# Fewer blocks first, a product pass of four tiles, and mixing on VectorE in a fused RWKV-5 and shrink-MLP kernel

## The chip, the cores and the metric

The kernel runs on one core of a Trainium2 chip. The metric is the device time of one execution in microseconds (us); lower is better. A core has five engines that run their own instruction streams: TensorE (PE, matmuls; its weight loads are listed as PEld), VectorE (DVE), ScalarE (ACT), GpSimd (POOL) and SyncE (SP, which here only issues transfers). The profile is that of one execution.

## The reference

All arithmetic is float32. `r`, `k`, `v` are (4, 8, 768, 48): 4 sequences, 8 heads, 768 steps, 48 per head.

```python
# first block: a decayed linear attention with a bonus for the own step
for t in range(S):
    cur = einsum('bhd,bhe->bhde', u[None] * k[:, :, t], v[:, :, t])
    y[:, :, t] = einsum('bhd,bhde->bhe', r[:, :, t], state + cur)
    state = w[None, :, :, None] * state + einsum('bhd,bhe->bhde', k[:, :, t], v[:, :, t])
x = y.transpose(0, 2, 1, 3).reshape(3072, 384)
# second block, w_in (384, 2048) and w_out (2048, 384), both given as float64
h = x @ w_in
out = (h - tanh(h)) @ w_out
```

## The kernel before, in words

**Units.** The first block is cut into 24 units of 64 steps of two sequences with all heads. For a unit SyncE loads r, k and v; TensorE transposes r and k (`turn`), multiplies the two for the levels (`levels`, with the state's part in `from_state`), VectorE masks the levels (`x.cp`, a predicated copy, L892), ScalarE writes the diagonal (`diagonal`), and TensorE multiplies by v (`outputs`) and updates the state (`to_state`), all of them recorded on L693. ScalarE copies the result to `xt`, and GpSimd issues small transfers that move the rest into place (`fill`). The first units have TensorE banks of their own (`x_ps`); the later ones, called `two` in the code, share one pair of banks (`yk_ps`), so their steps follow one another more strictly.

**Blocks and tiles.** Two units make a block of 256 rows of x; there are 12 blocks. The second block of the reference runs block by block over 8 tiles of 256 columns of w_in. A tile is: h, two halves of three matmuls each (L166); five ScalarE steps on 128x512 (`s`, `th`, `tg`, `q`, `small`); four VectorE steps on 128x512 (`g`, `c1`, `c2`, `cp`, L190 to L196), which make g = h - tanh(h) with a series where h is small; and the multiplication of g by its rows of w_out. A tile does this plainly (`o`, L204: four matmuls of 384 columns) or with seven products for eight (`products`, L254): g is cut into four 128x128 squares and w_out into 192-column halves, as in Strassen's scheme in Winograd's form; seven matmuls of 192 columns take the place of eight. The products need three sums of the squares of g (`sums_of_g`, GpSimd, L239 to L243) and four combinations of the squares of w_out (`mix`, GpSimd, L263, sixteen instructions for all of w_out, made once). `collect` (L275, L284) combines the seven results after a block's last tile.

**Passes.** The first FIRST = 6 blocks go through the tiles in four passes of two tiles each (PASSES = 4, 4, 4, 4 counts columns of 128), so that work can begin while w_in and w_out are still on their way; a block's sums wait in `part` (L217 adds them up). The other six blocks go through all eight tiles at once with `products`, except the last two tiles of the last block (ALONE = 4), which are plain.

**Weights.** w_in and w_out come as 64-bit words in 16 pieces; VectorE (L135, L136, L139 to L141, on 128x768) and ScalarE (L137, L138) convert each piece, and four staging buffers hold pieces on the way. The products' combinations lie where the staging buffers were, so mixing waits for all 16 conversions (`converted` in `mixing`).

**Order.** Nothing runs in the order in which the code names it. `Plan` holds every step with an engine, an assumed cost, what it waits for and a due time; `forward` lists the steps by due time on each engine, `order` searches over due times, and the steps are then issued in the order of the best plan. The plan also assumes when TensorE's own instructions arrive (`step`, `bound`, `comes`), and puts filler matmuls that compute nothing of use into the gaps at the start (`fills`, `filled`; L630 and L631), so that TensorE's clock stays up. In `order` the gaps are computed a second time, from a step's start and cost.

Of the kernel before, what the change touches and what calls it, by code (L numbers as in the profile page):

```python
# [34 lines left out]
L = 2  # L35
FIRST = 6
PASSES = 4, 4, 4, 4
OWN = 1
SWAP = 2
ALONE = 4  # L40
# [103 lines left out]
class Dense:  # L144
# [62 lines left out]
    def empty(self, t, i):  # L207

        whole, at = t.fs[1] == self.d.NF, (t.j, i)
        if t.fs[0]:  # L210
# [3 lines left out]
            if i and t.j in self.negative:  # L214
                self.nc.vector.tensor_tensor(t.o, part, self.outs[i], ALU.subtract)
            else:
                self.nc.vector.tensor_tensor(t.o, self.outs[i], part, ALU.add)  # L217
# [39 lines left out]
    def mix(self, f, x):  # L257
# [5 lines left out]
        self.nc.gpsimd.tensor_tensor(pairs[:, :, out], a, b, op)  # L263

    def collect(self, t, x):

        n, ps, V = self.d.DM // 2, self.seven.ps, self.nc.vector
        if x == 0:
            t.e, t.u = (self.work.tile([128, self.d.DM], F32, name=name, tag="part", bufs=L * FIRST) for name in "eu")
            whole = t.fs[1] == self.d.NF  # L270
            t.os = [self.work.tile([128, self.d.DM], F32, name="o", tag="o") if whole else
                    self.work.tile([128, self.d.DM], F32, name="part", tag="part", bufs=L * FIRST) for _ in range(L)]
            if not whole:
                self.sums.update({(t.j, i): t.os[i] for i in range(L)})
            self.nc.scalar.copy(t.e[:, :n], ps[0][:, :n])  # L275
        else:
# [7 lines left out]
            V.tensor_tensor(out, x, y, op)  # L284

# [10 lines left out]
class Plan:  # L296
# [33 lines left out]
    def forward(self, due):  # L330
# [7 lines left out]
        starts, done, last, first, changed = [None] * len(ready), [], 0.0, {}, set(waiting)  # L338
        while len(done) < len(ready):
# [21 lines left out]
            if e == "PE":  # L361
                if filling:
                    step += 4 * len(self.filled(filling, free[e], start, starts))
# [72 lines left out]
    def order(self, tries=1000):  # L436
# [24 lines left out]
        free, order, fills = self.BEGIN["PE"], [], iter(self.fills)  # L461
        filling = next(fills, None)
        for t in done:
            t.start = starts[t.n]
            if t.engine == "PE" and filling:
                order += [SimpleNamespace(engine="PE", cost=0.0, start=free, run=run)
                          for run in self.filled(filling, free, t.start, starts)]
                if t is filling[1]:
                    filling = next(fills, None)
                free = t.start + t.cost  # L470
# [21 lines left out]
def near(ctx, tc, r, k, v, w, u, out, shared, moe_w_in, moe_w_out):  # L492
# [75 lines left out]
    def new_outs(t):  # L568
        if t.j >= FIRST:
            return [x[:, : d.DM] for x in dense.seven.ps[:L]]  # L570
# [22 lines left out]
    dense.negative = set(range(FIRST, d.NB))  # L593
# [34 lines left out]
    def fills(to):  # L628
        wide = w_up.rearrange("d p z t -> d (p z t)")
        return [(.9, lambda: T.matmul(to, ident, wide, start=True, stop=True)),  # L630
                (.25, lambda: T.matmul(to[:, :128], ident, ident, start=True, stop=True))]  # L631
# [280 lines left out]
    def mixing():  # L912

        for f in range(0, d.NF // 2, 2):
            now = None
            for x in range(4):
# [4 lines left out]
                now = add("POOL", 1.0, run, converted + [now])  # L921
            mixed.append(now)

    def finished_seven(t, x, due, pace):

        whole, now, steps, j = t.fs[1] == d.NF, x.o, [], t.j
        for i, (e, cost) in enumerate((("ACT", .3), ("DVE", .26), ("DVE", .26), ("DVE", .26), ("DVE", .26), ("DVE", .47), ("DVE", .26))):
            now = add(e, cost, lambda i=i: dense.collect(t, i), [now] + (sum((stored.get((j - 1, i), []) for i in range(L)), []) if whole and not i else []), due + 3 * pace)
            steps.append(now)
        x.empty, x.emptied = steps[:4], steps[4:]  # L930
        if whole:
            for i in (1, 0):
                stored[j, i] = [add("POOL", .6, lambda z=z, i=i: dense.store(t.os[i], L * j + i, z, G),
                                    [steps[4 if i else 6]], due + 4 * pace, data=.4) for z in range(2)]

    def hidden(j, fs, f, due, pace, seven=False):
# [10 lines left out]
        if m == 0:  # L947
            plan.fills += [([], tabled, fills(idle)[1:]), ([ups], now, fills(idle))]
# [9 lines left out]
        if seven:  # L958
# [4 lines left out]
            now = add("PE", 1.32, lambda: dense.products(t, 0), [x.sg, mixed[f // 4], b1.o, done.cp, done.diag, done.lev] + b1.empty, due + 2 * pace, steps=16)  # L963
            x.o = add("PE", .99, lambda: dense.products(t, 1), [now] + b1.emptied, due + 2 * pace + 1.3, steps=12)
            if t.last:
                finished_seven(t, x, due, pace)
# [360 lines left out]
```

## Time and profile before

| | |
|---|---|
| Median of the runs | 617.49 us (3 runs, 616.53 to 619.28) |
| The profiled execution | 616.69 us, its span 615.0 us |
| Mean granted TensorE clock | 0.991 |
| TensorE busy | 596.4 us (97%) |
| Weight loads (PEld) | 483.4 us (79%) |
| VectorE busy | 453.5 us (74%) |
| ScalarE busy | 401.9 us (65%) |
| GpSimd busy | 177.1 us (29%) |
| h, L166 | 282.4 us busy, 1152 records |
| Plain w_out, L204 | 142.0 us busy, 384 records of 400 |
| Seven products, L254 | 158.6 us busy in four groups, 644 records |
| Mixing, L263 | 22.0 us busy in three groups, 16 instructions |

A float32 matmul shows as two records. A group's busy time is the time in which at least one of its records runs; records of matmuls overlap, so the time that one takes is read from start to start. A busy TensorE need not be at its peak. A few matmul records are missing. Timeline lines give start and length in us, engine, line, operation, output and inputs, shapes and count; in brackets the idle time before and what ended it. Lines of stretches give, for each engine, busy us and count, then TensorE's granted clock, the busy share of the transfer engines and GB/s.

### The profile page before, as it was taken

The numbers are of one execution on the slowest core, as the hardware profiler recorded it, in microseconds if no ns is written. First come the engines' busy times: TensorE is split into PE (matmuls) and PEld (weight loads), VectorE is DVE, ScalarE is ACT, GpSimd is POOL, SyncE is SP. The second block draws the span as 40 slices with busy tenths as digits, with TensorE's granted clock in tenths as the row PEclk, the third lists the DMA queues.
The fourth block names the chain that finished last, engine by engine and source line by source line (L and its number), as shares of the span: only waits on it lengthen the run. The fifth ranks groups of instructions, "written<-read, shape, count | busy, mean of one in ns | idle before, by whom it ended". The sixth has DMA issues, their size and how long they took to land.

```text
span 615.0 us, 13927 instructions
## 1 busy us (share of the span) xinstructions
PE 596.4 (97%) x5499; PEld 483.4 (79%) x5499; DVE 453.5 (74%) x735; ACT 401.9 (65%) x896; POOL 177.1 (29%) x313
## 2 busy tenths in 40 slices
PE   8799999999999999997999999999999999999995
PEld 7477777667777777775777799889889899889993
DVE  5599888997789689996668765766786765645753
ACT  2498878878676567662557765675775666747652
POOL 5001311300000000193123452543362244436440
PEclk9899999999999999997999999999999999999999
DMA  7964686407024100002123410130120010100101
GB/s 128 219 126 88 129 161 166 90 0 174 8 46 102 52 0 2 0 14 52 38 52 82 82 23 0 37 57 19 26 58 17 15 27 7 23 6 8 26 2 30
DMA packets 86323, 33.73 MB, mean 55 GB/s; under 512 B 78537, under 2 KB 80681, under 8 KB 86249
## 3 DMA queue, kind: packets, MB, share of 16 engines
q1 hardware_dynamic: 81084, 25.57, 20.7%
q0 software_dynamic: 4992, 6.99, 5.2%
q8 instruction: 45, 0.74, 0.5%
q14 instruction: 30, 0.24, 0.1%
q10 hardware_dynamic: 172, 0.20, 0.1%
HBM read 26.94 MB, written 4.72 MB: 51 GB/s over the span
## 4 chain that ended last, share of the span: by engine, by line
PE 79%; DVE 9%; ACT 5%; issue 3%; DMA 2%; SPq 1%; DVEq 0%; ACTq 0%
PE h L166 36%; PE p L254 17%; PE o L204 16%; PE yk_ps L693 5%; DVE rT L742 1%; DVE tg L194 1%; PE yk_ps L738 1%; DVE tg L192 1%; PE h L630 1%; SPq L726 1%; ACT at L763 1%; PE p L204 1%; PE x_ps L738 1%; DVE g L196 1%; DMA kt<-in_k_dram 1%
## 5 line engine op out<-in xcount | busy, mean ns | idle before, releaser
L166 PE MATMUL h<-xt,w_in_sb 128*128 128x256 f32 x1152 | 282.4, 382 | 0.2 <-DVE w_in_sb L141 0.2
L166 PEld LDWEIGHTS h<-xt,w_in_sb 128*128 128x128 f32 x1152 | 214.6, 191 | 42.7 <-issue 1.0
L204 PE MATMUL o<-w_out_sb,g 128*128 128x384 f32 x384 | 142.0, 493 | 0.5 <-DVE g L196 0.3
L192 DVE SCALAR_TENSOR_TENSOR tg<-s,tg 128x512 f32<-128x512 f32 x96 | 68.7, 716 | 58.8 <-ACT tg L179 44.4
L190 DVE TENSOR_TENSOR g<-h,th 128x512 f32<-128x512 f32 x96 | 65.9, 686 | 43.0 <-ACT s L175 32.2
L204 PEld LDWEIGHTS o<-w_out_sb,g 128*128 128x128 f32 x384 | 72.0, 191 | 32.5 <-DVE g L196 1.4
L179 ACT ACTIVATE tg<-h 128x512 f32<-128x512 f32 x96 | 57.2, 595 | 53.7 <-PE h L166 53.7
L175 ACT ACTIVATE s<-h 128x512 f32<-128x512 f32 x96 | 57.3, 596 | 49.7 <-PE h L166 49.7
L177 ACT ACTIVATE th<-h 128x512 f32<-128x512 f32 x96 | 57.1, 595 | 32.0 <-PE h L166 31.9
L196 DVE COPY_PREDICATED g<-small,tg 128x512 f32<-128x512 int32 x96 | 73.2, 763 | 5.0
L194 DVE SCALAR_TENSOR_TENSOR tg<-q,tg 128x512 f32<-128x512 f32 x96 | 69.6, 725 | 6.1 <-ACT q L181 2.6
L239 POOL TENSOR_TENSOR sg<-g 128x256 f32<-128x256 f32 x46 | 35.2, 766 | 132.3 <-DVE g L196 123.0
L181 ACT ACTIVATE q<-s,m1b 128x512 f32<-128x512 f32 x96 | 69.5, 724 | 0.5
L183 ACT ACTIVATE small<-s,smallb 128x512 f32<-128x512 f32 x96 | 69.4, 723 | 0.5
L254 PE MATMUL p<-mixed,sg 128*128 128x192 f32 x276 | 67.4, 326 | 0.0
L850 POOL DMA_DIRECT2D xt<-rest x66 | 32.4, 497 | 91.8 <-ACT rest L829 91.6
L763 ACT ACTIVATE at<-same,du 128x64 f32<-128x64 f32 x184 | 47.6, 341 | 4.9 <-DVE du L759 4.7
L254 PEld LDWEIGHTS p<-mixed,sg 128*128 128x128 f32 x276 | 48.7, 190 | 0.0
L254 PE MATMUL p<-w_out_sb,g 128*128 128x192 f32 x184 | 46.2, 333 | 0.0
L254 PEld LDWEIGHTS p<-w_out_sb,g 128*128 128x128 f32 x184 | 33.2, 190 | 4.3
L263 POOL TENSOR_TENSOR mixed<-w_out_sb 128x384 f32<-128x384 f32 x8 | 10.9, 1378 | 77.2 <-DVE w_out_sb L141 77.2
L829 ACT COPY xt<-yk_ps 64x192 f32<-64x192 f32 (+2 forms) x50 | 16.2, 323 | 23.7 <-PE yk_ps L693 23.3
(136 smaller groups left out, 694.4 us busy)
## 6 DMA issues: line engine op xcount, KB each, us to landing
st<-in_moe_w_out_dram SPq DMA_DIRECT2D x8, 768.0 KB, 7.3
rt<-in_r_dram SPq DMA_DIRECT2D x48, 96.0 KB, 2.9
vt<-in_v_dram SPq DMA_DIRECT2D x48, 96.0 KB, 3.0
st<-in_moe_w_in_dram SPq DMA_DIRECT2D x16, 288.0 KB, 6.4
kt<-in_k_dram SPq DMA_DIRECT2D x44, 96.0 KB, 2.9
out_dram<-part POOLq DMA_DIRECT2D x24, 96.0 KB, 2.2
out_dram<-o POOLq DMA_DIRECT2D x20, 96.0 KB, 2.1
st<-in_moe_w_in_dram POOLq DMA_DIRECT2D x16, 96.0 KB, 3.9
```

Source lines behind the costliest of these rows:

```text
L166: self.nc.tensor.matmul(t.h2[:, z], self.w_in_sb[:, t.f // 2, kk, z * 128 : (z + 1) * 128], self.xts[t.j][:, kk].rearrange("p b t -> p (b ...
L175: A.activation(out, t.h, AF.Square)
L177: A.activation(out, t.h, AF.Tanh)
L179: A.activation(out, t.h, AF.Tanh, scale=G1)
L181: A.activation(out, t.s, AF.Square, bias=self.m1b)
L183: A.activation(out, t.s, AF.Relu, bias=self.smallb, scale=-1.0)
L190: V.tensor_tensor(t.g, t.h, t.th, ALU.subtract)
L192: V.scalar_tensor_tensor(t.tg, t.s, C4, t.tg, ALU.mult, ALU.mult)
L194: V.scalar_tensor_tensor(t.tg, t.q, K1, t.tg, ALU.add, ALU.mult)
L196: V.copy_predicated(t.g, t.small.bitcast(I32), t.tg)
L204: self.nc.tensor.matmul(self.outs[i], t.g2[:, z, i * C : (i + 1) * C], self.w_out_sb[:, t.f + z, :], start=t.first and z == 0, stop=t.last ...
L254: self.nc.tensor.matmul(ps[bank][:, half * n : (half + 1) * n], a, b, start=t.first and half == 0, stop=t.last, skip_group_check=True)
```

## The change

It has six parts.

1. FIRST goes from 6 to 5. PASSES become 4, 4, 8: two passes of two tiles and one of four. In that last pass (columns from SEVEN = 8 on) the tiles use `products`. The sums of the first two passes wait in `part` as before, and a new function `gather` adds them to what `collect` makes of the third.
2. ALONE goes from 4 to 2: one plain tile at the end instead of two.
3. Mixing runs on VectorE instead of GpSimd, and is planned ahead of the passes, since the third pass needs it.
4. `collect` starts after the first four of a tile's seven products, and has its own buffers `e` and `u`. The products of the next tile wait for its first four steps, not for all.
5. A filler is 512 or 256 columns of the identity (before: 512 of the decay table, once that was there, or 128 of the identity), from the first instruction on. `order` takes the fillers from the plan that it chose (`fitted`), instead of computing the gaps again.
6. All blocks keep the second half of their x negated (`negative`), as the seven products want it; plain parts undo the sign when they are whole.

With it the first 14 units (before: 16) use the separate banks, and 10 (before: 8) share one pair. Of the 96 tiles 21 are plain (before: 50) and 75 use products (before: 46).

```diff
-FIRST = 6
-PASSES = 4, 4, 4, 4
+FIRST = 5
+PASSES = 4, 4, 8
-ALONE = 4
+ALONE = 2
+SEVEN = 8
...
-            if i and t.j in self.negative:
+            if i and whole and t.j in self.negative:
...
-        self.nc.gpsimd.tensor_tensor(pairs[:, :, out], a, b, op)
+        self.nc.vector.tensor_tensor(pairs[:, :, out], a, b, op)
...
+    def gather(self, t, i):
+        self.nc.vector.tensor_tensor(t.os[i], t.os[i], self.sums.pop((t.j, i)), ALU.subtract if i else ALU.add)
...
-                    step += 4 * len(self.filled(filling, free[e], start, starts))
+                    runs = self.filled(filling, free[e], start, starts)
+                    self.fitted.append((free[e], t.n, runs))
+                    step += 4 * len(runs)
...
-            if t.engine == "PE" and filling:
-                order += [SimpleNamespace(engine="PE", cost=0.0, start=free, run=run)
-                          for run in self.filled(filling, free, t.start, starts)]
-                if t is filling[1]:
-                    filling = next(fills, None)
-                free = t.start + t.cost
+            free, runs = fitted.get(t.n, (0.0, [])) if t.engine == "PE" else (0.0, [])
+            order += [SimpleNamespace(engine="PE", cost=0.0, start=free, run=run) for run in runs]
...
-    dense.negative = set(range(FIRST, d.NB))
+    dense.negative = set(range(d.NB))
...
-        wide = w_up.rearrange("d p z t -> d (p z t)")
-        return [(.9, lambda: T.matmul(to, ident, wide, start=True, stop=True)),
-                (.25, lambda: T.matmul(to[:, :128], ident, ident, start=True, stop=True))]
+        def run(n):
+            T.matmul(to[:, : n * 128].rearrange("p (n m) -> p n m", n=n), ident, ident[:, None, :].to_broadcast([128, n, 128]),
+                     start=True, stop=True)
+        return [(.9, lambda: run(4)), (.46, lambda: run(2))]
...
-                now = add("POOL", 1.0, run, converted + [now])
+                now = add("DVE", .47, run, converted + [now])
...
+            before = sum((stored.get((j - 1, i), []) for i in range(L)), []) if not i else [x.o] if i == 4 else []
+            now = add(e, cost, lambda i=i: dense.collect(t, i), [now] + before, due + 3 * pace)
             steps.append(now)
-        x.empty, x.emptied = steps[:4], steps[4:]
+        x.empty, x.emptied = steps[:2], steps[2:]
...
+            if t.fs[0]:
+                now = add("DVE", .47, lambda i=i: dense.gather(t, i), [now], due + 3 * pace)
...
-            plan.fills += [([], tabled, fills(idle)[1:]), ([ups], now, fills(idle))]
+            plan.fills.append(([], now, fills(idle)))
...
-            now = add("PE", 1.32, lambda: dense.products(t, 0), [x.sg, mixed[f // 4], b1.o, done.cp, done.diag, done.lev] + b1.empty, due + 2 * pace, steps=16)
+            now = add("PE", 1.32, lambda: dense.products(t, 0), [x.sg, mixed[f // 4], b1.o, done.cp, done.diag, done.lev] + b1.empty + b1.emptied[:2], due + 2 * pace, steps=16)
...
-                hidden(j, (done, done + part), f, now, pace)
+                hidden(j, (done, done + part), f, now, pace, done >= SEVEN)
```

## The prediction, made before the changed kernel ran

> **What bounds the kernel now.** I read the page's shares first (TensorE 97% busy, VectorE 74%, ScalarE 65%, GpSimd 29%), then the slices, because an average hides stages.
>
> ```profile
> PE   8799999999999999997999999999999999999995
> PEclk9899999999999999997999999999999999999999
> ```
>
> TensorE is full from the third slice on, except in the nineteenth, where its granted clock falls too. So time is TensorE's instructions, plus a few holes. Five places matter: the start (to 53 us, where the first w_out matmul stands), the hole near 283 us, the plain stage, the stage with products, the tail. Busy times by stretch, columns as in the page (PE, PEld, DVE, ACT, POOL, clock, DMA share, GB/s):
>
> ```profile
> 53.00:258.00 205.00, 203.62 (x1704) 150.25 (x1704) 177.29 (x287) 154.06 (x334) 18.62 (x38) 1.00 0.34 73
> 280.00:285.00 5.00, 1.65 (x42) 1.07 (x44) 4.74 (x8) 0.00 (x0) 1.54 (x3) 0.83 0.10 22
> 285.00:290.00 5.00, 5.00 (x44) 3.43 (x37) 1.12 (x2) 2.52 (x10) 1.03 (x2) 0.50 0.66 130
> ```
>
> From 53 to 258 us TensorE lacks only 1.4 us, but VectorE works 86% of it too: it also converts the weights. The hole, in the timeline:
>
> ```profile
> 258.96 2.73 POOL L263 TENSOR_TENSOR mixed<-w_out_sb 128x384 f32<-128x384 f32 x2 [77.16 <-DVE w_out_sb L141]
> 259.52 1.30 DVE L194 SCALAR_TENSOR_TENSOR tg<-q,tg 128x512 f32<-128x512 f32 x1
> ...
> 283.93 1.14 PE L693 MATMUL yk_ps<-at,vt 64*64 64x64 f32 x32 [3.35 <-DVE at L892]
> ```
>
> While the sixteen mixing instructions run on GpSimd (259 to 280 us, 22 us in all) VectorE's 512-wide steps take 1.3 to 1.5 us instead of 0.69. VectorE falls behind, TensorE waits 3.35 us, and then runs at half clock for 6.25 us, which costs another 3.1. The start and the tail:
>
> ```profile
> 20.20 0.77 PE L693 MATMUL x_ps<-rT,kT 48*64 48x64 f32 x26 [3.70 <-issue]
> 20.91 6.90 PE L630 MATMUL h<-w_up,ident 128*128 128x512 f32 x12
> ...
> 31.25 0.69 DVE L742 TENSOR_TENSOR rT<-x_ps,w_up 128x512 f32<-128x512 f32 x1 [3.48 <-ACT kT L751]
> ...
> 604.69 5.63 PE L204 MATMUL p<-w_out_sb,g 128*128 128x384 f32 x16 [1.66 <-DVE e L284]
> ```
>
> TensorE stands 3.7 us for nothing that the profile shows (my reading: its own instructions had not come), and then works off six filler matmuls in 6.9 us, half of them at half clock, though the operands of the next real matmuls were ready at 22.2. VectorE pays for it with 3.48 us of waiting.
>
> **The change, part by part.**
>
> *Products.* Steps from start to start:
>
> ```profile
> 348.19 1.45 PE L204 MATMUL o<-w_out_sb,g 128*128 128x384 f32 x4
> 349.48 1.46 PE L166 MATMUL h<-xt,w_in_sb 128*128 128x256 f32 x6
> 350.77 0.49 PE L254 MATMUL p<-w_out_sb,g 128*128 128x192 f32 x2
> ...
> 352.07 1.46 PE L166 MATMUL h<-xt,w_in_sb 128*128 128x256 f32 x6
> 353.37 0.49 PE L254 MATMUL p<-w_out_sb,g 128*128 128x192 f32 x2
> ...
> 354.34 1.46 PE L166 MATMUL h<-xt,w_in_sb 128*128 128x256 f32 x6
> ```
>
> Half a plain w_out tile takes 1.29 us, so a tile 2.58; four products take 1.30 and three 0.97, so a tile 2.27. Plain tiles go from 50 to 21 (20 in passes one and two, one at the end), product tiles from 46 to 75: 29 x 0.31 = **-9.0 us**. [...]
>
> Per product tile GpSimd adds three sums of g (0.77 + 0.53 + 0.56 = 1.86 us) in a period of 4.86: hidden, 177 busy us become about 209. Without that cover (sums later than the next half of h, 1.29 us) each tile would pay the excess. The cross-block collects on VectorE: six more at 1.78 (four 192-wide at 0.26 plus 0.26 and 0.47), ten gathers, minus 26 plain adds at 0.47: +3.2 us, and they lie in the product stage, where VectorE is 65% busy. A collect now starts after the first four products, and the next tile's first products wait for four of its steps (about 1.4 us) while three products and two halves of h (3.6 us) run: nothing. The ScalarE copy that begins a collect waits for the previous block's stores (2.1 us to land) with the next tile's tanh behind it, but blocks are 19 us apart: nothing.
>
> *Mixing on VectorE.* Sixteen instructions at the 0.47 of a 384-wide step, 7.5 us, and VectorE's other steps keep 0.61. The hole of 3.35 and its half clock go: **-6.4 us**. This holds where the hole stood; the mixing itself moves, see the third part.
>
> *Start.* Fillers become wide ones from the first instruction, and are set by what the plan assumed, so the six at 20.9 us become single ones. Against this, five 512-wide fillers now stand ahead of the transpose of decay and bonus (5.24 us before). A filler takes 0.86 us at full clock and 1.7 at half; a 128-wide one took 0.47 us from 1.5 us on and 0.22 from 7.8 on, so I put the rise near 6.9, and the five end near 8.5 and that transpose comes near 9.0, 3.7 us late. Stepping through the order, the second unit's first level matmuls then stand near 19.3 instead of 16.2. Before, they waited there until 20.2 anyway, so this costs nothing as long as the instructions arrive by then; bounds 0 to +5. After it one filler (0.9, cold 1.7) instead of 6.9 us lets the first half of h start near 26 instead of 30.9. From there VectorE sets the pace (21.4 of 22 us busy from 31 to 53): its order has 18.3 us of steps to the end of the first tile, so 45.5, and the first w_out matmul near 46.5 instead of 53.1: **-6.6 us**, between 0 and -9.
>
> *Earlier products: VectorE's queue.* All sixteen weight pieces and the first mixing must now be done before the first product, which moves from tile 49 to tile 21, while TensorE's work up to there shrinks. Steps of VectorE:
>
> ```profile
> 252.84 0.96 DVE L139 SCALAR_TENSOR_TENSOR w_out_sb<-w_out_sb,st 128x768 f32<-128x768 uint32 x1
> 253.70 0.69 DVE L194 SCALAR_TENSOR_TENSOR tg<-q,tg 128x512 f32<-128x512 f32 x1
> 254.30 0.56 DVE L217 TENSOR_TENSOR part<-o,part 128x384 f32<-128x384 f32 x1
> 254.77 0.95 DVE L140 SCALAR_TENSOR_TENSOR power<-st,power 128x768 uint32<-128x768 uint32 x1
> ```
>
> 0.86 for 768 wide, 0.60 to 0.61 for 512, 0.65 for a predicated copy, 0.47 for 384. Between the first tile's last step and the masking of unit 13 (the fourteenth), whose banks the products take over, VectorE's instructions in the order built from the changed program are 94 x 0.47 + 75 x 0.61 + 31 x 0.65 + 39 x 0.86 = 143.7 us. TensorE has, from its first w_out matmul to the first product, 132 x 0.431 (h) + 80 x 0.647 (w_out) + 608 small at 0.033 and 72 transposes at 0.11 = 136.7, and about 0.45 per unit for changes of shape (68.0 us measured for 63.5 of such work between the first and ninth tile), so 141. VectorE is the longer. Counted the same way, before had 173.0 us of VectorE steps in 205.8 us (84%), but there TensorE set the pace. Where VectorE was pressed it was 97% busy (31 to 53, 60 to 70 us). I take 96%: 149.7, so the first product near 195.2 instead of the 187.5 of TensorE alone: **+7.7 us**; bounds 0 (it keeps up) and +29 (84%). These gaps should be short and many. [...] One long gap would add 3 us, short ones nothing, and I take nothing.
>
> *Rest.* The small waits of 53 to 258 us (1.4) are inside the last item: -1.4. Two more units run with one shared bank pair in the product stage, where a unit cost 0.85 of changes (259.1 us from the first product to the end, for 250.6 of steps and the hole of 1.66, over eight units) instead of 0.45: +0.8. In the tail the last tile's chain (4.6 us from the end of h to its mask, as now) outlasts the 3.25 us of products left: a hole of 1.4 instead of 1.66: -0.3.
>
> **Sum**: -9.0 - 6.4 - 6.6 + 7.7 - 1.4 + 0.8 - 0.3 = -15.2. The profiled execution took 616.7 (span 615.0): 601.5; the median of the runs shown is 0.8 above it: **602.3 us**.
>
> **Rivals.**
> 1. *VectorE's queue becomes the bound and the kernel is slower.* Place: the first product. If VectorE gets through its 143.7 us at 84%, that product stands at 45.5 + 171 = 216.5, 21.3 later, total 623.6. For it: the 84%, and ScalarE, which shares the chain, was 86% busy from 31 to 121 us. Against: 97% where pressed. It decides below 143.7 / (149.7 + 15.2) = 87%.
> 2. *The hole wasn't the mixing's.* It is the long VectorE chain of a unit (masking behind four tile steps), and comes back before the first product with its half clock: +6.4, 608.7. For it: that unit waits at the head of TensorE's queue. Against: VectorE's doubled steps from 259 to 280.
> 3. *The start gains nothing.* The late transpose and the late instructions add up, the first w_out matmul stays near 53: 608.9. For it: the filler sum above. Against: VectorE's 3.48 us wait goes.
> 4. *VectorE keeps up* at 100%: 594.6.
>
> **How the numbers follow.** Forecast 0.50 (597 to 608), rival 4 0.14, rivals 2 and 3 together 0.24 (606 to 614), rival 1 0.12, of which two thirds end slower. A difference under 0.5% (3.1 us) can't be told from none here. Slower: 0.08; within: 0.05, the mild end of rival 1 and of 2 and 3 together; faster: 0.87. The range for 8 in 10 leaves out rival 1 and the best of rival 4: 594 to 613.
>
> **What would show it.** First w_out matmul near 46.5; first product near 195 with VectorE over 94% busy from 46 to 195 and TensorE's idle there 6 to 10 us in short gaps, ended by VectorE; no half clock after 30 us; product tiles at 4.86 from there on; 1.4 us of hole before the last w_out matmuls. Wrong if TensorE's idle before the first product is over 15 us or under 2, or if the first tile is not earlier.

## The result, and the profile after

| | before | after |
|---|---|---|
| Median | 618.27 us (4 runs, 616.53 to 619.28) | 610.81 us (4 runs, 610.4 to 611.83) |
| After to before | | 0.9885 (95%: 0.9856 to 0.9913) |
| Profiled execution, its span | 616.69, 615.0 us | 610.4, 608.7 us |
| TensorE / VectorE / GpSimd busy | 97 / 74 / 29% | 96 / 76 / 35% |
| First w_out matmul | 53.09 | 50.60 |
| First product | 350.77 | 197.59 |
| End of the last matmul; from there to the end of the span | 610.32; 4.65 us | 601.23; 7.45 us |

The kernel became 7.5 us faster; 15.2 were forecast (602.3 for 617.5). The time lies in the range of 594 to 613, and the sign was right, but half of the forecast gain isn't there; the range was wide enough for that, which is no merit of the working. Measured against the sum's own execution (a span of 599.8), 8.9 us are missing, and they can be placed:

| stretch | forecast | measured | difference |
|---|---|---|---|
| to the first w_out matmul | 46.5 | 50.6 | +4.1 |
| from there to the first product | 148.7 | 147.0 | -1.7 |
| from there to the end of the last matmul | 399.95 | 403.64 | +3.7 |
| from there to the end of the span (forecast as before) | 4.65 | 7.45 | +2.8 |

The slices of the changed kernel's page, busy TensorE and its granted clock in tenths:

```profile
PE   9789889999999989999999999999999999999994
PEclk9799999999999999999999999999999999999998
```

The hole in the nineteenth slice and its half clock are gone. In their place the third, fifth and sixth slices (30 to 46 and 61 to 91 us) are less full than the slices of before from the third on. TensorE's timeline at the start and at the first block with products (start, length, then as before):

```profile
1.52 6.01 PE L632 MATMUL h<-ident 128*128 128x512 f32 x10 [1.52 <-POOL ident masks.py:199]
...
7.90 0.23 PE L640 MATMUL yk_ps<-ident,rows 8*128 8x8 f32 x1
...
18.50 0.70 PE L632 MATMUL h<-ident 128*128 128x512 f32 x1
22.96 1.22 PE L632 MATMUL h<-ident 128*128 128x512 f32 x1 [3.76 <-issue]
...
29.45 1.46 PE L167 MATMUL h<-xt,w_in_sb 128*128 128x256 f32 x6
...
50.60 1.53 PE L205 MATMUL o<-w_out_sb,g 128*128 128x384 f32 x4 [0.76 <-DVE g L197]
```

```profile
197.59 0.59 PE L255 MATMUL p<-w_out_sb,g 128*128 128x192 f32 x2 [0.29 <-DVE at L896]
...
218.45 0.59 PE L255 MATMUL p<-w_out_sb,g 128*128 128x192 f32 x2 [0.93 <-DVE e L283]
...
220.18 0.59 PE L255 MATMUL p<-mixed,g 128*128 128x192 f32 x2 [0.81 <-DVE o L283]
```

The 3.7 us in which TensorE waits "for nothing that the profile shows" are still there, in the middle of one filler, and the first half of h comes at 29.45 instead of the forecast 26. At the end of the first block with products, TensorE waits 1.74 us for `collect`. The forecast had put the price of that wait at nothing: some 1.4 us of VectorE's steps against 3.6 us of TensorE's own work, with VectorE 65% busy in the stage with products. The stretches show why that average misled (columns as before):

```profile
200.00:225.00 25.00, 23.26 (x124) 21.15 (x123) 24.58 (x42) 13.81 (x31) 11.39 (x18) 1.00 0.08 17
225.00:250.00 25.00, 24.90 (x134) 23.01 (x133) 22.48 (x36) 14.83 (x28) 13.31 (x21) 1.00 0.11 25
250.00:275.00 25.00, 25.00 (x135) 23.31 (x134) 18.02 (x29) 16.21 (x30) 12.14 (x21) 1.00 0.08 17
```

VectorE is full until about 225 and 90% busy to 250, since mixing (185 to 211 us), the first collects and a unit meet there. The tail:

```profile
594.65 0.45 POOL L244 TENSOR_TENSOR sg<-sg,g 128x128 f32<-128x128 f32 x1
...
598.38 2.85 PE L205 MATMUL p<-w_out_sb,g 128*128 128x384 f32 x8 [0.36 <-DVE e L283]
```

The hole before the last w_out matmuls is 0.36 us (1.4 were forecast). But the span ends 7.4 us after the last matmul. In the trace's own records, which the page doesn't list since such steps don't count as busy, GpSimd has a last step (a drain) of 10.37 us after its last sum: from 597.48 to 607.84 in the changed kernel, from 599.77 to 610.14 before. Before, the other engines were done at 613.85 and GpSimd waited for them. After, they are done at 604.86 and wait 3.0 us for GpSimd.

### The profile page after: what moved, and what is told of

It reads as the page before. It is cut to its first block, busy times and chain, and to the rows that moved or that the text cites. A ratio compares the mean times of both kernels' runs of the same rounds, so it can differ in the third digit from the quotient of the medians.

```text
span 608.7 us, 14333 instructions
## 1 busy us (share of the span) xinstructions
PE 584.0 (96%) x5617; PEld 497.8 (82%) x5617; DVE 465.0 (76%) x771; ACT 403.4 (66%) x902; POOL 211.3 (35%) x384
## 4 chain that ended last, share of the span: by engine, by line
PE 69%; DVE 12%; ACT 8%; issue 7%; POOL 1%; DMA 1%; DVEq 0%; POOLq 0%; ACTq 0%
PE h L167 32%; PE p L255 24%; PE yk_ps L697 4%; PE o L205 4%; PE h L632 2%; DVE tg L193 1%; DVE tg L195 1%; DVE g L197 1%; DVE rT L746 1%; DVE g L191 1%; ACT th L178 1%; PE yk_ps L742 1%; ACT at L767 1%; POOL xt L854 1%; ACT s L176 1%
## 5 line engine op out<-in xcount | busy, mean ns | idle before, releaser
L240 POOL TENSOR_TENSOR sg<-g 128x256 f32<-128x256 f32 x75 | 57.0, 759 | 197.6 <-DVE g L197 142.6
L255 PE MATMUL p<-mixed,sg 128*128 128x192 f32 x450 | 110.1, 326 | 0.0
L255 PEld LDWEIGHTS p<-mixed,sg 128*128 128x128 f32 x450 | 79.3, 190 | 0.2 <-issue 0.2
L255 PE MATMUL p<-w_out_sb,g 128*128 128x192 f32 x300 | 74.9, 332 | 1.3 <-DVE e L283 0.9
L197 DVE COPY_PREDICATED g<-small,tg 128x512 f32<-128x512 int32 x96 | 71.2, 742 | 4.3
L255 PEld LDWEIGHTS p<-w_out_sb,g 128*128 128x128 f32 x300 | 54.9, 190 | 9.5 <-DVE e L283 1.3
L205 PE MATMUL o<-w_out_sb,g 128*128 128x384 f32 x160 | 59.1, 492 | 2.0 <-DVE g L197 1.2
L244 POOL TENSOR_TENSOR sg<-sg,g 128x128 f32<-128x128 f32 x75 | 44.4, 592 | 5.4
L205 PEld LDWEIGHTS o<-w_out_sb,g 128*128 128x128 f32 x160 | 29.3, 190 | 15.7 <-PE x_ps L632 1.6
L242 POOL TENSOR_TENSOR sg<-sg,g 128x128 f32<-128x128 f32 x75 | 40.2, 535 | 5.4
```

The source lines that it names most:

```text
L197: V.copy_predicated(t.g, t.small.bitcast(I32), t.tg)
L205: self.nc.tensor.matmul(self.outs[i], t.g2[:, z, i * C : (i + 1) * C], self.w_out_sb[:, t.f + z, :], start=t.first and z == 0, stop=t.last ...
L255: self.nc.tensor.matmul(ps[bank][:, half * n : (half + 1) * n], a, b, start=t.first and half == 0, stop=t.last, skip_group_check=True)
```

## The experiments

For comparison across kernels I split each profiled span into four parts. "Needed" is TensorE's instructions without fillers, at one duration for each kind (h 0.431, plain w_out 0.647, small 0.033 and transposes 0.110 us as in the prediction, a product 0.326). What is over before the first product (fillers, idle time, half clock, changes of shape) and after it is the rest of those stretches, and the last column is from the last matmul to the end.

| kernel | needed | over, before the first product | over, after it | end | span |
|---|---|---|---|---|---|
| before | 554.0 | 47.4 | 8.9 | 4.7 | 615.0 |
| after | 545.1 | 42.3 | 13.9 | 7.4 | 608.7 |
| after, profiled again (e15) | 545.1 | 44.7 | 13.9 | 7.2 | 610.9 |
| e4, mixing on GpSimd | 545.1 | 45.0 | 9.1 | 7.7 | 606.8 |
| e6, third pass plain | 551.2 | 38.7 | 9.8 | 8.1 | 607.8 |
| e9, VectorE relieved, planned | 545.0 | 39.5 | 10.8 | 7.6 | 602.9 |
| e10, VectorE relieved later | 545.1 | 42.0 | 10.9 | 7.4 | 605.3 |
| e11, old fillers and last sums | 545.1 | 41.2 | 12.6 | 4.8 | 603.5 |

Two profiles of the changed kernel differ by 2.4 us before the first product, so a difference of that size there proves nothing by itself. A second caution: where an experiment is "planned anew", `order` searches again (1000 random shifts, from a fixed start), so any change in what it is told can lead to another order of everything. e3, e4, e5, e6, e7, e8 and e9 are of this kind; e1, e2, e10, e13 and e14 keep the order of the changed kernel. No run changed the search alone, so what a new order is worth by itself isn't known; e3 and e7, whose edits concern the fillers of the start, gained 2.9 and 3.0 us. Ratios are to the kernel before on the same chip, with their 95% intervals.

**The end: e1, the last sums on VectorE.** The three sums of g of the last tile that uses products move; nothing else does.

```diff
-        add, g, s = self.nc.gpsimd.tensor_tensor, ...
+        add, g, s = (self.nc.vector if t.j == self.d.NB - 1 and t.f == self.d.NF - ALONE - 2
+                     else self.nc.gpsimd).tensor_tensor, ...
```

> The changed kernel with one edit: the three sums of g of the very last tile that uses products are made on VectorE instead of GpSimd; the planned order is kept. Theory (GpSimd's end): in the changed kernel GpSimd's last sum ends at 595.1, and after it stands a step of 10.37 us at its end, so that the program closes at 608.7, 3.0 us after the other engines are done. With the edit GpSimd is done one tile (4.9 us) earlier and no longer last: from the last matmul to the end of the span about 4.5 us instead of 7.5. The 0.8 us of sums that VectorE gets lie ahead of the last plain tile's steps, so up to 0.8 more of a hole there. Median near 608.2 (607.5 to 609). Rival (the end waits for the landing of the last transfers, or for SyncE): no gain, 610.8 to 611.6.

Measured: 609.25 us, ratio 0.9834 (0.9809 to 0.986). From the last matmul to the end it is 4.7 us; GpSimd's drain, again 10.37 us, runs from 594.69 to 605.06. So the place is confirmed. The median fell by 1.6 us (2.0 against the repeat, e15), less than the expected 2.6, and the interval touches that of the changed kernel; the profiled execution started later (first w_out matmul at 52.25) and hides the gain in its span. The same edit was made on two other kernels, below (e11, e12).

**VectorE's queue: e2, two of its steps left out in tiles 3 to 21.**

```diff
-        elif x == "c1":
+        elif x in ("c1", "c2") and getattr(t, "few", False):
+            return
+        elif x == "c1":
...
+        t.few = 2 <= m < 21
```

> The changed kernel with two of the four VectorE steps (c1 and c2) left out in tiles 3 to 21, so the small-h branch of their g is wrong; everything else and the planned order are kept. 38 steps of 0.61, 23 us of VectorE's work before the first product. Theory (VectorE's queue sets the first product, the step of +7.7): from the first w_out matmul to the first product 141 us instead of 147.0, VectorE well under 90% busy there, the total 6 us down, near 605. Rival (another chain, ScalarE's or the loads', sets it, or the queue would cost nothing): under 1.5 us, 609 to 611.

Measured: 611.9 us, ratio 0.9872 (0.9844 to 0.99); 150.2 us from the first w_out matmul to the first product in the profile, which is of the slowest of the four runs and holds two spells at half clock there (granted clock 0.95 from 60 to 80 us, 0.88 from 80 to 100). Read alone, this rejects the theory: 23 us less for VectorE, and no gain. TensorE is idle for 5.4 us in that stretch (5.1 in the changed kernel), though VectorE is busy for 82% of it instead of 97%. The longest of these waits shows what holds it:

```profile
74.69 0.58 ACT L757 COPY kT<-x_ps 128x512 f32<-128x512 f32 x1
75.31 0.69 DVE L748 TENSOR_TENSOR rT<-x_ps,w_up 128x512 f32<-128x512 f32 x1 [2.10 <-ACT kT L757]
...
76.85 0.55 DVE L862 TENSOR_TENSOR state<-yk_ps,state 128x384 f32<-128x384 f32 x1
77.45 0.88 PE L699 MATMUL yk_ps<-rT,state 48*64 48x64 f32 x32 [2.23 <-DVE state L862]
```

VectorE itself stands for 2.10 us, until ScalarE has made `kT`, and the `state` for which TensorE waits comes behind that in VectorE's order. In the changed kernel the same wait of TensorE is 1.76 us, with VectorE idle for only 0.42. So under this order less load on VectorE leaves the wait where it is. But the engines run their instructions in the planned order, and that order was made for a VectorE with those steps in it.

**e9, the same with the plan told of it** (cost 0.02 for these steps, so that the order is made anew).

> As the second experiment (c1 and c2 left out in tiles 3 to 21, so that part of the result is wrong), but the plan knows it (cost 0.02 instead of 0.6 each), so that the order of all engines is fitted to a VectorE with 23 us less to do. If VectorE's load before the first product costs TensorE time and only the fixed order hid that in the second experiment: TensorE's time before the first product that isn't needed work, 42 us in the changed kernel, falls to about 36, total 603 to 606. If the load of VectorE there costs nothing: 40 to 45 us, total 608.5 to 612.

Measured: 604.0 us, ratio 0.9754 (0.9719 to 0.9789). From the first w_out matmul to the first product it takes 140.3 us where TensorE alone had been worked out at 141 (6 matmuls of h, 2.6 us, moved behind that product, though). "Over, before the first product" is 39.5 us (36 expected), and "after it" 10.8 instead of 13.9. That is 6.8 us by the medians, and 5.9 by these two columns. Not all of it need be VectorE's: the order is a new one, and the new orders of e3 and e11 have 12.1 and 12.6 us after the first product without any relief for VectorE. What lies before the first product (2.8 us) is hardly more than the 2.4 between two profiles of one kernel. So VectorE's load costs up to some 6 us of the span with an order made for it; that e2 showed nothing because of its fixed order is likely, and not shown apart from the search. The stretches from 53 to 197.5 and from 197.5 to 250 us, after and then e9:

```profile
53.00:197.50 144.50, 139.51 (x1660) 104.48 (x1651) 140.62 (x236) 120.00 (x278) 19.76 (x38) 1.00 0.49 102
...
197.50:250.00 52.50, 50.58 (x266) 46.27 (x266) 49.56 (x81) 31.14 (x62) 25.98 (x40) 1.00 0.09 20
```

```profile
53.00:197.50 144.50, 142.12 (x1660) 106.24 (x1659) 133.81 (x219) 120.07 (x283) 20.77 (x40) 1.00 0.55 108
...
197.50:250.00 52.50, 52.50 (x281) 48.96 (x280) 38.63 (x62) 32.11 (x58) 24.02 (x41) 1.00 0.07 16
```

TensorE's idle time falls from 5.0 to 2.4 us in the first and from 1.9 to 0 in the second, while VectorE's busy share falls from 97 to 93% and from 94 to 74%.

**e10, the steps left out in tiles 20 to 33** (`t.few = 19 <= m < 33`, order kept): the beginning of the products alone.

> The changed kernel with c1 and c2 left out in tiles 20 to 33 (part of the result is wrong), the planned order kept: 17 us less for VectorE from about 180 to 250 us, where mixing, the first units in the shared banks and the first collects meet. Theory (VectorE's queue at the beginning of the products makes the 1.74 us of waiting at the first block's end and most of the 1.9 of small waits after it): TensorE from the first product to its last matmul 403.7 down to about 401, total near 608.3. Rival (the collect's chain of steps is too long in itself, whatever VectorE's load): 403.5 again, total 610 to 611.5.

Measured: 607.03 us, ratio 0.9808 (0.9773 to 0.9843). From the first product to the last matmul it takes 400.7 us instead of 403.6; in its trace TensorE isn't idle at all between 197.5 and 250:

```profile
197.50:250.00 52.50, 52.50 (x282) 49.09 (x281) 37.69 (x63) 33.46 (x65) 24.90 (x41) 1.00 0.09 20
```

So 3.0 of the missing 3.7 us of this stretch are VectorE's queue at the beginning of the products, and the collect's chain isn't too long in itself. The order was kept and the intervals of the two kernels don't overlap, so this is the clearest evidence of VectorE's part.

**Mixing: e4, back on GpSimd in the changed kernel.**

```diff
-        self.nc.vector.tensor_tensor(pairs[:, :, out], a, b, op)
+        self.nc.gpsimd.tensor_tensor(pairs[:, :, out], a, b, op)
...
-                now = add("DVE", .47, run, converted + [now])
+                now = add("POOL", 1.0, run, converted + [now])
```

> The changed kernel with mixing put back on GpSimd (cost 1.0 in the plan, as before); planned anew. Theory (while GpSimd mixes, VectorE's steps take about twice as long): VectorE, which sets the first product, gives up 7.5 us of mixing and loses about 11 us over GpSimd's 22: first product 3 to 10 us later than 197.6, with a hole and perhaps a spell at half clock as before at 283; total 614 to 622. Rival (VectorE is simply relieved): first product near 192, total 603 to 606.

Measured: 608.17 us, ratio 0.9819 (0.9798 to 0.9839): neither theory; it is faster than the changed kernel, and the intervals don't overlap. Both effects are there. VectorE's steps do stretch while GpSimd mixes (the predicated copy below takes 1.35 us, the one at 178.53, ahead of the mixing, 0.74), and TensorE waits for them:

```profile
198.09 2.40 POOL L264 TENSOR_TENSOR mixed<-w_out_sb 128x384 f32<-128x384 f32 x2
...
200.34 0.59 PE L255 MATMUL p<-w_out_sb,g 128*128 128x192 f32 x2 [1.83 <-DVE at L896]
...
201.15 1.35 DVE L197 COPY_PREDICATED g<-small,tg 128x512 f32<-128x512 int32 x1
```

From 180 to 200 us TensorE is idle 3.8 us, and the first product comes at 200.3. But after it no wait at the block's end is left, and "over, after it" is 9.1 instead of 13.9 us. In this order, relief where VectorE's queue is fullest is worth more than the stretched steps cost; the order is a new one too, and e8 (below) doesn't bear the gain out.

**e5, mixing on VectorE alone, in the kernel before** (the same two lines the other way round).

> The kernel before with one part of the change alone: mixing on VectorE (cost 0.47 in the plan), still needed only by the seventh block; planned anew. Theory of the prediction: the hole of 3.35 us near 283 us and the half clock after it were GpSimd's mixing; both go, -6.4: about 612 (610 to 614) where before is 618.3. Rival 2 (the hole is the unit's own chain and stays): 616 to 619.

Measured: 613.27 us, ratio 0.9909 (0.9882 to 0.9936), 5.4 us faster than before beside it. From the first w_out matmul to the first product it takes 291.4 us instead of 297.7, which is the forecast 6.4; the start of this execution was 1.7 later. No half clock is left after 26 us, and TensorE is full where the hole was:

```profile
250.00:300.00 50.00, 50.00 (x312) 36.50 (x309) 36.25 (x63) 28.83 (x55) 4.21 (x8) 1.00 0.12 24
```

So the hole was the mixing's (rival 2 falls). The same edit gains 5.4 us where VectorE has slack around it; where it hasn't, the changed kernel is 2.6 us slower than e4, with the order as a second difference.

**Products: e6, the third pass plain again.** Half of the rows of the first five blocks get part of their sum with the wrong sign in this kernel, which costs no time.

```diff
-SEVEN = 8
+SEVEN = 99
```

> The changed kernel with the third pass (four tiles of each of five blocks) plain again; products only from the sixth block on; planned anew. TensorE then has 20 tiles at 2.58 instead of 2.27, +6.2 us; nothing else that TensorE does changes. Theory after the second experiment (VectorE's load before the first product costs TensorE nothing in sum): 610.8 + 6.2, less up to 1.7 for the wait at the first block's end with products: 615 to 617. The prediction's step (early products cost 7.7 through VectorE's queue): 610.8 + 6.2 - 7.7, about 609.3.

Measured: 610.85 us, ratio 0.9883 (0.985 to 0.9917): the same time as the changed kernel, though TensorE has 6.1 us more to do. What the twenty early product tiles save comes back: 3.6 us before the first product and 4.1 after it (table above), less 0.7 at the end; the new order may have some 3 us of this. Where e6's products begin, TensorE waits for nothing: by then VectorE has converted all weights and made all mixtures, and it is busy for 65% of the time:

```profile
296.00:321.00 25.00, 25.00 (x195) 22.93 (x194) 16.25 (x26) 15.62 (x37) 11.56 (x21) 1.00 0.15 29
```

**The start: e3, no filler ahead of TensorE's first needed instruction, and e7, the fillers of before.**

```diff
-            plan.fills.append(([], now, fills(idle)))
+            plan.fills.append(([cols], now, fills(idle)))
```

> The changed kernel with one edit: no filler may stand ahead of the transpose of decay and bonus (TensorE's first needed instruction); the order is planned anew. Theory (instructions are fetched by TensorE's own progress): TensorE stops at its 240th weight load in both kernels known (16.24 to 20.20 before, 18.50 to 22.96 after), so an earlier start moves the stop forward as a whole: the transpose near 5.3 instead of 7.9, the stop about 2.5 earlier and still 3.7 to 4.5 long, first w_out matmul near 48.3 instead of 50.6, total near 608.5. Rival A (the fillers up front pay by the clock: without them more work runs at half clock): first w_out at 50 to 52, total 610 to 612. Rival B (the stop goes away with the fillers, since fewer instructions come before): first w_out near 45, total near 605.

Measured (e3): 607.92 us, ratio 0.9823 (0.9803 to 0.9842). The total was hit, but not by the expected steps: the transpose came at 3.63, the stop for instructions shrank to 0.9 us from weight load to weight load, and the first w_out matmul came at 54.8, because the new plan put other work ahead of it. "Over, before the first product" is 41.0 us, "after it" 12.1: the 1.8 us won after it are the new plan's, far from the edit.

For e7, `fills` and its two lists are those of the kernel before, used with `fitted`:

```diff
-            plan.fills.append(([], now, fills(idle)))
+            plan.fills += [([], tabled, fills(idle)[1:]), ([ups], now, fills(idle))]
```

> The changed kernel with the fillers of before (128 wide early, 512 wide of the decay table later), still taken from the chosen plan; planned anew. Theory (five wide fillers ahead of TensorE's first needed instruction delay it and with it the stop for instructions): the transpose of decay and bonus near 5.3 instead of 7.9 to 8.7, the stop after the same 219th recorded weight load but earlier (reached near 16.3), total 1 to 3 us down, 608 to 610. Rival (the new fillers brought the 2.5 us by which the first w_out matmul came earlier): back to 53 us there, total near 613.

Measured (e7): 607.78 us, ratio 0.9825 (0.9791 to 0.9859). Transpose at 4.81, first w_out matmul at 48.65: the rival falls, and the new fillers didn't bring the start's gain. How much of the 3.0 us is the fillers' and how much the new order's isn't told apart.

**e13, the five first fillers dropped, e14, all fillers dropped, both with the order kept, and e15, the changed kernel beside them.**

```diff
+            runs = [] if free == self.BEGIN["PE"] else runs     # e13
+            runs = []                                           # e14
             order += [SimpleNamespace(engine="PE", cost=0.0, start=free, run=run) for run in runs]
```

> The changed kernel, its order kept, without the five 512-wide fillers at TensorE's very start. The transposes of the first r come first then (with their load, near 6.3), decay and bonus near 6.6 instead of 7.9. Theory (the fillers delay the start, and the stop for instructions comes at a fixed count of instructions): the stop now falls ten weight loads later in the work, is reached near 16.5 to 17.5 and ends near 20 to 21.5, the first w_out matmul near 49 and the total 1 to 2 us under the changed kernel's beside it. Rival (instructions come at one time, near 23, whatever TensorE does): no gain, within 0.7 us of it. Rival (without these fillers the clock rises later and work runs at half clock for it): 1 to 3 us slower.

> The changed kernel, its order kept, without any filler. If the fillers earn their place by the clock: TensorE at half clock for most of the first 40 us and some spells to 60, 5 to 10 us slower than the changed kernel. If what sets the start is the chain through VectorE and the arrival of instructions, with TensorE in slack: within 2 us of it. The stop after the 219th weight load falls 20 or more loads later in the work, and is reached near 15 to 17.

> The changed kernel itself, on the same chip as the two others: 610.8 (609.5 to 612), first w_out matmul at 50.4 to 52.3, the stop after the 219th recorded weight load, 7.4 us from the last matmul to the end.

Measured: e13 610.64 us, ratio 0.9864 (0.9831 to 0.9897); e14 612.51, 0.9884 (0.9851 to 0.9916); e15 611.23, 0.9871 (0.9848 to 0.9893). The three can't be told apart by time. Without any filler the median is 1.3 us up, which is within what can't be told, where 5 to 10 us had been thought possible; its mean granted clock was 0.979 to 0.988 in the four runs, for 0.991 to 0.994 in e15. The start of e13:

```profile
6.22 0.27 PE L641 MATMUL yk_ps<-ident,rows 8*128 8x8 f32 x1
...
21.83 0.40 PE L698 MATMUL yk_ps<-at,vt 64*64 64x64 f32 x13 [1.57 <-issue]
...
26.48 1.53 PE L167 MATMUL h<-xt,w_in_sb 128*128 128x256 f32 x6 [0.87 <-DVE w_in_sb L142]
...
48.08 1.53 PE L205 MATMUL o<-w_out_sb,g 128*128 128x384 f32 x4 [0.76 <-DVE g L197]
```

With those five fillers gone, h begins at 26.5 and the first w_out matmul stands at 48.1, near the forecast 26 and 46.5. Only the fillers were taken out, so the late start of the changed kernel was theirs and that of the stop for instructions behind them (1.57 us here, 3.76 there); with one profile of e13, a part can be chance, since the stop ended 1.0 us apart in the two profiles of the changed kernel. Yet the first product of e13 stands at 197.1 (197.6 and 200.0 in the two profiles of the changed kernel): of 2.5 us won at the start, between 0.5 and 3.0 are left there, and in the time nothing that can be measured.

**e8, e11 and e12, edits together.**

> Three edits of the changed kernel at once: no filler ahead of the first transpose (third experiment), the last tile's sums on VectorE (first), mixing on GpSimd (fourth); planned anew. If the gains are of separate places (start, end, first block with products) they add: 610.8 - 2.9 - 2.6 - 2.6 = 602.7, and 602 to 605 with what a new plan shifts. If the third and fourth gain the same thing (less pressure before the first product), 605 to 607.

Measured (e8): 608.37 us, ratio 0.9834 (0.9806 to 0.9863); the gains don't add. From the last matmul to the end it takes 4.8 us, as it should, but the new plan has 14.2 us over after the first product (9.1 in e4): the gain of the fourth experiment didn't survive another order. Against e12 (below), which differs by mixing on VectorE and the order for it, e8 is 2.0 us slower, with intervals that overlap. So on which engine mixing is better at this place stays open.

> The seventh experiment (fillers of before) with the first's edit added, the last tile's sums on VectorE; the order is the seventh's. From the last matmul to the end 7.25 down to 4.6, up to 0.8 of it lost in the tail's hole: 607.8 - 2.2 = about 605.5 (604.5 to 606.5). If the end were not GpSimd's: 607 to 609.

> The third experiment (no filler ahead of the first transpose) with the last tile's sums on VectorE; the order is the third's. From the last matmul to the end 8.1 down to 4.6: 607.9 - 3.0 = about 605 (604.3 to 606). If the end were not GpSimd's: 607 to 609.

Measured: e11 605.57 us, ratio 0.9791 (0.9754 to 0.9827), end 4.8 us; e12 606.39 us, ratio 0.9788 (0.9747 to 0.9829), end 5.7 us. Against the kernels of the same order (e7, e3) the last sums on VectorE bring 2.2 and 1.5 us (2.1 and 2.2 by the ratios, which allow for the chip); the intervals overlap, and the shorter ends (7.3 to 4.8 and 8.1 to 5.7 us) are what shows it. e11 and e12 are faster than both the kernel before and the changed one; which of the two is better isn't decided.

## Why the prediction was wrong by half, and where it was right

Three steps failed, and each has its size: the start, where the instructions came too late (h 3.5 us later than forecast); VectorE's queue after the first product, put at nothing (3.0 us); and GpSimd's last step at the end, which the sum left out (2.8 us). The time fell where rivals 2 and 3 were put (606 to 614), but not by their ways: rival 2 falls by e5, and the start gave 2.5 us where rival 3 has none. Term by term:

- *Products, -9.0.* Right in TensorE's work: needed time fell from 554.0 to 545.1, and tiles with products take 4.87 us. The share of weight loads rose from 79 to 82% of the span, and no tile got longer for it (4.86 us before). But the 6.1 us of the early products bring no time in all (e6, up to what its new order is worth).
- *Mixing, -6.4.* Right for the hole (5.4 measured alone, with 4.0 to 7.3 as its interval; 6.3 in the traces). The prediction said that "the mixing itself moves, see the third part"; where it moved to, at the beginning of the products, it meets a full VectorE. Whether GpSimd would have done it more cheaply there is open: 2.6 us by e4, the reverse by e8 and e12.
- *Start, -6.6.* Wrong: 2.5. The step that failed: "this costs nothing as long as the instructions arrive by then; bounds 0 to +5". They didn't arrive, and h came at 29.45 instead of 26, inside those bounds: TensorE stopped behind the weight load at 18.50 for 3.76 us, then had half clock until 28.38. The trace of before had shown the same stop, and I had read it as a fixed time (20.2) that a later start would meet; in the runs it is a place in the instruction stream (after the 220th recorded weight load in thirteen of 17 profiles), and the time at which TensorE goes on from there was later here, for a reason that is only partly known (last section). One reading of that trace was off as well: of the six fillers at 20.9 about two ran at half clock (3.0 of 6.9 us), not half. Dropping the five first fillers alone brought h to 26.5 (e13).
- *VectorE's queue, +7.7.* The time fits: 147.0 us from the first w_out matmul to the first product, 149.4 in the second profile, for 148.7; TensorE idle 5.1 and 5.8 us of it (6 to 10 were forecast), VectorE 96 to 97% busy. That VectorE's load makes these waits is only partly shown: under the kept order they stayed without 23 us of it (e2), and they fell to 2.2 us in the new order of e9. That the early products cost 7.7 us by e6 is chance, since the term was meant for the stretch before the first product and e6 finds 3.6 there. Wrong in place: I ended the queue at the first product. It lasts 50 us longer, and 3.0 us of it (e10) are the term that was missing. The sentence that failed is that the collects "lie in the product stage, where VectorE is 65% busy", and that the wait for four of their steps costs "nothing".
- *Short gaps, nothing for the clock.* So it was before (1.4 us of small waits from 53 to 258 us, at a clock of 1.00) and in the first profile of the changed kernel (1.00 from 28.38 us to the last matmul), but not in the second: in e15 the clock was 0.50 from 78.56 to 81.97, behind waits of 1.77 and 0.41 us, which costs 1.7 us (half of the 3.41).
- *Tail, -0.3.* The hole was better than forecast (0.36 for 1.4), but GpSimd's drain was overlooked, +2.8. ALONE = 2 puts GpSimd's last sum one tile nearer to the end. In the kernel before, the drain ended 3.7 us ahead of the other engines, too little for a tile of 4.87, and it can be read in the trace of before. e1 took it away: 4.7 us from the last matmul to the end instead of 7.4.

The misses: +4.1 at the start, +3.7 after the first product (3.0 of them VectorE's), +2.8 at the end, -1.7 before the first product (+0.7 in the second profile).

## What to carry to other kernels

Cost a moved step against the busy share of the engine in the very stretch where it lands, not in its stage: the collects were put at nothing by an average of 65%, and cost 3.0 us where VectorE was 94% busy. When the order comes from a search, an edit that makes it search again changes two things at once, and here that could be worth as much as the edit; experiments that keep the order, such as e10 and e1, are the ones that prove. Under a kept order, though, taking load from an engine shows nothing where that engine itself waits in the order, as in e2: look at what the wait ends on before rejecting. Look at what each engine does after its last useful instruction before shortening the end.

## What the runs showed of the hardware

**Half clock came in spells of 3.41 us or a multiple, behind stretches of 3.41 us in which TensorE was busy for less than about half.** In all 17 profiles the spells at half clock were that long (3.41 and 6.83 us before, 6.83 in the changed kernel), but for those that the program's start or end cuts. I divided each span into stretches of 3.41 us, laid so that the clock's changes fall between them, and set TensorE's busy share in one beside the clock in the next: of 2,889 stretches at full clock (without the one at each program's end), all 23 with a share under 0.465 were followed by half clock, none of the 41 between 0.535 and 0.70, six of the eight in between, and one of the 2,817 above. The shares ahead of the spells within the span were 0.09 and 0.19 before and 0.31 in the changed kernel. In e15:

```profile
75.15:78.56 3.41, 1.24 (x66) 1.09 (x65) 3.41 (x8) 3.38 (x7) 0.00 (x0) 1.00 0.80 144
78.56:81.97 3.41, 3.41 (x28) 1.73 (x32) 3.14 (x5) 2.57 (x8) 0.00 (x0) 0.50 0.01 3
```

and in e1, where a stretch was 57% busy, none followed:

```profile
91.42:94.84 3.42, 1.94 (x34) 1.63 (x27) 3.06 (x5) 1.31 (x5) 1.01 (x2) 1.00 0.70 95
94.84:98.25 3.41, 3.41 (x20) 2.62 (x18) 1.90 (x4) 3.36 (x9) 0.00 (x0) 1.00 0.95 198
```

In the 3.41 us from 75.15 in e15 TensorE was idle for 2.17 us, in two waits of 1.77 and 0.41 us. In the changed kernel's first profile the same two waits took 1.76 and 0.40 us, but fell into two stretches (72.75 to 76.17 and 76.17 to 79.58 us, busy for 0.69 and 0.68), and the clock stayed at 1.00. So these waits cost 1.7 us in one profile and nothing in the other.

**GpSimd's drain at the end took 10.37 us in every profile of every kernel.** It begins 1.7 to 2.4 us behind the end of GpSimd's last operation. So in these kernels that operation has to end 12 to 13 us (the 10.37 and the 1.7 to 2.4) before the other engines are done, or the drain sets the end.

**TensorE's stop at the start came after the 219th or 220th weight load.** In thirteen of the 17 profiles TensorE stopped after the 220th recorded weight load, whatever that load was, and in three after the 219th (the expectations count from 0 and say 219th; the 240th of e3's is a miscount; e8 shows no stop there). It reached that place between 16.2 and 21.2 us and went on between 19.4 and 23.9, 1.3 to 2.0 us after the first 16 KB transfer of the queue of instructions had landed (18.45 and 20.21 us before, 21.34 and 22.96 in the changed kernel); from that load to the next it took 0.8 to 5.3 us. That the stop is a wait for instructions is my reading of these times. So in these runs other fillers moved the time at which it is reached and what is lost there, hardly the place. What sets the moment at which that transfer starts (16.6 to 21.0 us) stays open: it doesn't follow TensorE's progress alone, since e7 and e11, whose order on TensorE is the same up to there, differ by 2.5 us.
